# The values of chunk 0 first, from rows that are scaled but not shifted, with the shift's share added to KV as z times a row

## The chip, the cores and the metric

The kernel runs on one core of one Trainium2 chip. The metric is the device time of one launch, in microseconds (us). Every run also has a span, which is what the profiler saw and is about 1.8 us shorter, and a mean granted TensorE clock, where 1.0 is full speed. The experiments were timed in rounds beside fresh runs of the kernel before, on the chip of their batch.

A ratio is the mean time of one kernel's fast runs over the mean time of the other's fast runs of the same rounds. It is therefore not quite the ratio of the medians that are quoted.

Engines are called as the profile calls them: PE is TensorE (matmul), DVE is VectorE, ACT is ScalarE, POOL is GpSimd, SP is SyncE, which issues most of the DMA here.

## The reference, cut to what matters

```python
mod = (silu(c) @ w_mod).reshape(1, 6, 1, 1024)
sa, ca, ga, sb, cb, gb = ...                 # six rows of 1024
h = layernorm(x) * (1 + ca) + sa             # x: 2048 x 1024, "scale" ca and "shift" sa
q, k, v = h @ wqkv                           # 32 heads of 32
pq, pk = phi(q), phi(k)                      # phi(t) = where(t > 0, t + 1, exp(t)) + 1e-6
kv = einsum('bhsd,bhse->bhde', pk, v)        # per head 32 x 32, summed over all rows
z  = einsum('bhsd->bhd', pk)
o  = (pq @ kv) / (pq . z + 1e-6)
x  = x + ga * (o @ wo)
# then a second layernorm with cb, sb and a SwiGLU block of width 3584 (about 70% of PE's busy time)
```

The kernel works on four chunks of 512 rows, of four tiles of 128 rows each. A "group" is one 128 x 512 block of outputs: eight matmuls of 512 columns, one for each block of 128 inputs (`cc`). A chunk's keys are eight groups, and so are its values and its queries. I write K(2) for the keys of chunk 2, and so on.

## The kernel before: what the change and the argument touch

The loads are queued in the order in which the opening needs them. Keys come first, so the opening needs both scale and shift, of six of the eight blocks of columns, before any main matmul.

```python
    for k in range(DC // MP):                      # w_mod: scale (q=1) and shift (q=0), 768 of 1024 columns
        load_a(k, 1, nc.scalar if k == 0 else nc.sync)
        load_a(k, 0, nc.sync)
    # ... then wk, the fourth x tile, the other columns of w_mod, wv, x of chunk 1, wq
```

A tile's statistics run on DVE, its power of −1/2 and the small product `nmr` on POOL, the normalisation on ACT. The vector, scalar and POOL instructions of the opening are held in the order in which they are written:

```python
    def rstd_of(mv, n):
        # ... veps on DVE
        nc.gpsimd.tensor_tensor(out=rstd[:, 0:n], in0=veps[:, 0:n], in1=neg_half[:]..., op=ALU.pow)

    def normalise_act(dst, src, mv, rstd):
        # nmr = -mean * rstd on POOL, then
        nc.scalar.activation(out=dst, in_=src, func=ACT.Identity, bias=nmr[:], scale=rstd[:, 0:1])

    with in_order(nc.vector, nc.scalar, nc.gpsimd):
        # ...
        st0 = ln1_stats(0, 0)
        nc.vector.tensor_copy(out=sc32[:], in_=...)
        xns = [ln1_norm(*st0)] + [ln1_norm(*ln1_stats(0, t)) for t in range(1, 3)]
        # ... row products of scale and shift, transposes of three tiles, modulation of six blocks
        k_mms(0, gs, accs, 0, 5)                   # 30 main matmuls
        xn3 = ln1_norm(*ln1_stats(0, 3), dve=True)
        pe_transpose_tile(hT, xn3, 3)
        # ...
        k_mms(0, gs, accs, 5, A)
        mod_cols_b()                               # the other two blocks, 32 matmuls of one column
        # ... the rest of K(0)
```

The rest of the attention is a loop over chunks:

```python
    for sc in range(NSC):
        if sc > 0:
            k_phase(sc, 0, 2)
            kv_phase(sc - 1)                       # kvp: 128 small matmuls
            k_phase(sc, 2, 4)
            # ...
        v_phase(sc)
        if sc + 1 < NSC:
            with tc.issue_after(last_on[nc.vector.engine] if sc == 0 else last_phi[-5].ins):
                ln1(sc + 1)                        # next chunk; its tiles are transposed by DMA into hT
        # ...
    K_STEPS = [(), (2, 3), (0, 2), (0, 2, 4, 6)]   # behind which K groups a piece of the later modulation
    V_STEPS = [0, 4, 4, 6]                         # rows is summed on DVE, and how many during V
```

## Time and profile before

| | before |
|---|---|
| time, median of 3 (range) | 833.67 us (832.79 to 833.79) |
| span, granted clock | 831.0 us, 1.00 |
| last load that the first main matmul waits for | lands at 14.23 us |
| first main matmul (K of chunk 0) | 15.59 us |
| Q(0), V(1), V(2) start | 44.49, 73.38, 102.55 us |

From the page of the kernel before, first the busy time of each engine, then the chain of work that ended last by engine:

```profile
PE 819.9 (99%) x4502; PEld 378.9 (46%) x4581; DVE 344.5 (41%) x659; ACT 168.5 (20%) x253; POOL 64.3 (8%) x166
...
PE 97%; DMA 2%; issue 1%; DVE 0%; ACTq 0%; SPq 0%
```

PE is the limit everywhere except at the very start. So a change to the opening gains what it takes from the first 15.6 us, and any matmul added later costs its own length.

The chain of waits of the kernel before, in its first 19 us (start, length, what), shows what the opening waits for:

```profile
7.83 6.40 DMA wme<-in_w_mod_dram
14.23 0.04 issue
14.28 0.51 PE mod_ps L98 x8
14.79 4.21 PE acc L98 x19
```

It is a load of w_mod. After the last row products come four matmuls of zeros (1.04 us from 14.72) that keep PE busy while DVE modulates, and from 15.59 us the main matmuls follow one another. Here are the stages in PE's timeline of the kernel before (start, length, engine, line, operation, out<-in, size, count, and in brackets idle time before it):

```profile
15.59 6.64 PE L98 MATMUL acc<-wk,hT 128*128 128x512 bf16 x29
22.07 0.61 PE L101 MATMUL tp<-ident,xn 128*128 128x128 bf16 x8
...
44.49 13.98 PE L98 MATMUL acc<-hT,wq 128*128 128x512 bf16 x62
...
73.38 13.98 PE L98 MATMUL acc<-wv,hT 128*128 128x512 bf16 x62
87.19 3.75 PE L98 MATMUL acc<-wk,hT 128*128 128x512 bf16 x16
...
102.55 13.98 PE L98 MATMUL acc<-wv,hT 128*128 128x512 bf16 x62
```

None of these lines has idle time in brackets. The 30 matmuls from 15.59 us (one record is missing) hide the statistics and the normalisation of tile 3, whose transposes start at 22.07 us.

### The profile page before, as it was taken

Reading aid. Unit: us, or ns where it says so; the run is one execution under the profiler, and the core shown is the slowest. Engines: PE = TensorE matmul, PEld = TensorE weight load, DVE = VectorE, ACT = ScalarE, POOL = GpSimd, SP = SyncE. Lnnn points to the kernel's source line nnn. Section 1 sums busy time; section 2 is a strip of 40 time slices with the busy share of each in tenths; the row PEclk is TensorE's granted clock in tenths of the full one; section 3 lists DMA queues with packets and bytes.
Section 4 is the critical chain, followed back from the end, with each engine's and each line's share of the span. In section 5 each row is a group of like instructions: output and inputs, shape, how many; then the busy total and the mean of one; then the engine's idle time right before and its main releaser. Section 6 shows DMA issues by size and latency. Waiting matters only on the chain.

```text
span 831.0 us, 11112 instructions
## 1 busy us (share of the span) xinstructions
PE 819.9 (99%) x4502; PEld 378.9 (46%) x4581; DVE 344.5 (41%) x659; ACT 168.5 (20%) x253; POOL 64.3 (8%) x166
## 2 busy tenths in 40 slices
PE   8999999999999999999999999999999999999998
PEld 4444444444444444444444444444444444444444
DVE  5758879786354335421111354111114431111122
ACT  3455343434111111101111010111111101111000
POOL 2101020120221101100000010000001100000000
PEclk9999999999999999999999999999999999999999
DMA  9893964149986735646343183763405529710011
GB/s 324 296 203 65 194 150 102 37 101 326 375 204 219 227 121 169 160 153 211 110 146 108 54 221 92 249 195 100 153 1 174 152 68 345 231 45 0 19 58 51
DMA packets 144100, 129.07 MB, mean 155 GB/s; under 512 B 58608, under 2 KB 124656, under 8 KB 143536
## 3 DMA queue, kind: packets, MB, share of 16 engines
q1 hardware_dynamic: 139968, 114.97, 46.8%
q0 software_dynamic: 3792, 12.98, 4.9%
q8 instruction: 36, 0.59, 0.3%
q10 hardware_dynamic: 288, 0.40, 0.1%
q14 instruction: 16, 0.13, 0.0%
HBM read 101.98 MB, written 12.72 MB: 138 GB/s over the span
## 4 chain that ended last, share of the span: by engine, by line
PE 97%; DMA 2%; issue 1%; DVE 0%; ACTq 0%; SPq 0%
PE acc L98 90%; PE a_ps L98 7%; DMA wme<-in_w_mod_dram 2%; PE kvp L98 1%; PE wf L98 0%; PE den L98 0%; PE mod_ps L98 0%; ACTq L126 0%; PE tp L101 0%; SPq L135 0%; DVE e L698 0%; DVE ob L701 0%
## 5 line engine op out<-in xcount | busy, mean ns | idle before, releaser
L98 PE MATMUL acc<-h2T,wgu 128*128 128x512 bf16 x1755 | 385.6, 379 | 1.9
L98 PEld LDWEIGHTS <-wgu 128*128 128x128 bf16 x1792 | 175.3, 98 | 211.3
L677 DVE TENSOR_TENSOR gu<-acc,e 128x512 bf16<-128x512 f32 x112 | 77.4, 691 | 289.9 <-PE acc L98 278.8
L98 PE MATMUL acc<-wd,gu 128*128 128x512 bf16 (+2 forms) x908 | 195.2, 372 | 0.9
L676 ACT ACTIVATE e<-acc 128x512 f32<-128x512 f32 x112 | 66.9, 597 | 374.8 <-PE acc L98 363.4
L98 PEld LDWEIGHTS <-gu 128*128 128x128 bf16 x924 | 89.3, 98 | 104.4
L98 PEld LDWEIGHTS <-hT 128*128 128x128 bf16 x512 | 49.6, 98 | 59.8 <-DVE hT L237 0.9
L698 DVE TENSOR_TENSOR e<-acc,gb_bc 128x512 f32<-128x512 f32 (+2 forms) x33 | 22.3, 675 | 131.5 <-PE acc L98 122.5
L98 PE MATMUL a_ps<-wo,pq 128*128 128x512 bf16 x250 | 56.9, 379 | 0.3
L98 PE MATMUL acc<-wk,hT 128*128 128x512 bf16 x251 | 56.4, 379 | 0.5 <-issue 0.3
L98 PE MATMUL acc<-hT,wq 128*128 128x512 bf16 x249 | 55.8, 379 | 0.7 <-issue 0.5
L98 PE MATMUL acc<-wv,hT 128*128 128x512 bf16 x249 | 55.5, 379 | 0.4
L295 ACT ACTIVATE eb<-acc 128x512 bf16<-128x512 f32 x64 | 37.9, 596 | 75.4 <-PE acc L98 73.3
L234 ACT ACTIVATE xn<-x,nmr,rstd 128x1024 bf16<-128x1024 f32 x16 | 19.9, 1241 | 126.0 <-POOL nmr L232 126.0
L98 PEld LDWEIGHTS <-pq 128*128 128x128 bf16 x256 | 25.0, 98 | 30.2
L645 POOL DMA_DIRECT2D x_scratch<-x x16 | 9.8, 615 | 373.8 <-DVE x L638 373.6
L98 PEld LDWEIGHTS <-wq 128*128 128x128 bf16 x256 | 24.6, 98 | 29.8 <-issue 0.9
L296 DVE TENSOR_SCALAR eb<-eb 128x512 bf16<-128x512 bf16 x64 | 18.3, 290 | 31.2 <-ACT eb L295 31.0
L218 POOL TENSOR_TENSOR rstd<-veps,neg_half 128x1 f32<-128x1 f32 x32 | 17.8, 557 | 102.3 <-DVE veps L216 92.3
L638 DVE TENSOR_TENSOR x<-a_ps,x_sb 128x512 f32<-128x512 f32 x32 | 22.1, 690 | 8.6 <-PE a_ps L98 7.9
L701 DVE TENSOR_TENSOR ob<-e,x1r 128x512 bf16<-128x512 f32 (+2 forms) x33 | 22.3, 675 | 1.0
L639 DVE BATCH_NORM_STATS2 stats<-x 128x6 f32<-128x512 f32 x32 | 22.1, 693 | 1.0
(92 smaller groups left out, 295.9 us busy)
## 6 DMA issues: line engine op xcount, KB each, us to landing
wgu<-in_B_w_gate_dram SPq DMA_DIRECT2D x28, 1024.0 KB, 7.5
wgu<-in_B_w_up_dram SPq DMA_DIRECT2D x28, 1024.0 KB, 8.1
x_sb<-in_A_x_dram SPq DMA_DIRECT2D x32, 256.0 KB, 5.5
x_scratch<-x POOLq DMA_DIRECT2D x16, 512.0 KB, 3.4
x1r<-x_scratch SPq DMA_DIRECT2D x31, 256.0 KB, 2.7
wd<-in_B_w_down_dram SPq DMA_DIRECT2D x7, 1024.0 KB, 6.3
rbc<-rden_scratch POOLq DMA_DIRECT2D x16, 256.0 KB, 5.5
out_dram<-ob SPq DMA_DIRECT2D x31, 128.0 KB, 1.7
```

The source lines that it names most:

```text
L98: return tc.keep_in_program_order(nc.tensor.matmul(out, lhsT=lhsT, rhs=rhs, start=start, stop=stop))
L218: nc.gpsimd.tensor_tensor(out=rstd[:, 0:n], in0=veps[:, 0:n], in1=neg_half[:].to_broadcast([P, n]), op=ALU.pow)
L234: nc.scalar.activation(out=dst, in_=src, func=ACT.Identity, bias=nmr[:], scale=rstd[:, 0:1])
L295: nc.scalar.activation(out=e[:], in_=acc, func=ACT.Exp)
L296: nc.vector.tensor_scalar(out=e[:], in0=e[:], scalar1=1.0, scalar2=PHI_EPS, op0=ALU.min, op1=ALU.add)
L638: nc.vector.tensor_tensor(out=x1[:, ns], in0=a_ps[:], in1=x_t[:, ns], op=ALU.add)
L639: nc.vector.bn_stats(out=stats[:, nb, :], in_=x1[:, ns])
L645: nc.gpsimd.dma_start(out=x1_dram[st * P:(st + 1) * P, :], in_=x1[:])
L676: nc.scalar.activation(out=sg[:], in_=ps[0][:], func=ACT.Silu)
L677: gm = nc.vector.tensor_tensor(out=guT[sc][f // GPT][:, f % GPT, :], in0=ps[1][:], in1=sg[:], op=ALU.mult)
L698: nc.vector.tensor_tensor(out=yt, in0=y_ps, in1=gb_bc[:, ns], op=ALU.mult)
L701: nc.vector.tensor_tensor(out=ob, in0=yt, in1=x1r, op=ALU.add)
```

## The change

The values of chunk 0 come first. For them the rows are only scaled, `hs = xn * (1 + ca)`, so the opening needs half of w_mod's two blocks before its first main matmul. What is missing in V is the same row `vb = sa @ wv` on every line. In `kv = pk^T V` it adds up to `z0` times `vb`, where `z0` is the sum of `pk` over chunk 0. That is added to KV near 150 us. Keys and queries of chunk 0 use fully modulated rows as before.

The diff, cut to its core:

```diff
+    for j in range(DC):
+        load_block(wca, wm_v, j, D, nc.scalar if j == 0 else nc.sync)      # scale, 2.1 MB
+    for cc in range(DC):
+        load_block(wv, wqkv_v, cc, 2 * D)                                  # x tiles 2 and 3 in between
+    # ... shift (wsa), two x tiles of chunk 1, wk by blocks, the other two x tiles, wq
@@
-        st0 = ln1_stats(0, 0)
+        st0, st1 = ln1_stats(0, 0), ln1_stats(0, 1)
         nc.vector.tensor_copy(out=sc32[:], in_=...)
-        xns = [ln1_norm(*st0)] + [ln1_norm(*ln1_stats(0, t)) for t in range(1, 3)]
+        xn0, xn1 = ln1_norm(*st0), ln1_norm(*st1, dve=True)
@@
+        # ... row products of the scale, transposes of tiles 0 and 1
+        scale_to(hs, hT, 0, 0, H)                     # H: two tiles now, three before
+        # ... blocks 1 to 3
+        xn2 = ln1_norm(*ln1_stats(0, 2))
+        # ... blocks 4 to 7
+        gs = k_groups[0:4]
+        v_mms(hs, gs, accs, 0, 6)                     # 24 main matmuls
+        pe_transpose_tile(hT, xn2, 2)
+        for cc in range(DC):
+            scale_to(hs, hT, cc, H, H + P)
+        xn3 = ln1_norm(*ln1_stats(0, 3))
+        v_mms(hs, gs, accs, 6, DC)                    # 8 of them
+        v_mms(hs, gs2[0:1], accs2[0:1])               # 8 more
+        v_evac(0, gs, accs)
+        pe_transpose_tile(hT, xn3, 3)
+        for cc in range(DC):
+            scale_to(hs, hT, cc, H + P, SCW)
+        v_mms(hs, gs2[1:2], accs2[1:2])
+        mod_rows(0, 0, DC)                            # row products of the shift
+        # ... two more groups of V, then modulate_all(hT, ca1T, saT)
@@
-        v_phase(sc)
+        if sc == 0:
+            k_phase(0, 0, 8)
+        else:
+            v_phase(sc)
@@
     kv_phase(NSC - 1)
-    nc.vector.tensor_copy(out=KVB, in_=kv_acc[:, :, 0:DH])
+    vb = acc_b("vb", (HG, DH))
+    for cc in range(DC):
+        row_matvec(vb[:]..., sc32[:, cc, :], wv[cc // 4][:, cc % 4, :], cc == 0, cc == DC - 1)
+    # ... zb = vb * z0
+    nc.vector.tensor_tensor(out=KVB, in0=kv_acc[:, :, 0:DH], in1=zb, op=ALU.add)
```

(The folds of wo that follow are moved by one group of queries.)

More of the change, by code (lines that the diff above doesn't have):

```diff
@@ L122, in load_x @@
         x_tiles[st] = x_sb
-    for st in range(STC - 1):
+    for st in range(2):
         load_x(st, nc.sync)
     nc.scalar.dma_start(out=c_sb[:], in_=c_v)
-    wk = [big("wk", [4, D]), big("wk", [4, D])]
-    A, MP = 6, 2
-    AW, BW = A * P, (DC - A) * P
-    wma = [big("wme", [MP, 2, AW]) for _ in range(DC // MP)]
-    wmb = big("wme", [DC, 2, BW])
-    def load_a(k, q, eng):
-        eng.dma_start(out=wma[k][:, :, q, :], in_=wm_v[:, k * MP:(k + 1) * MP, q * D:q * D + AW])
-    def load_b(q, lo, hi):
-        nc.sync.dma_start(out=wmb[:, lo:hi, q, :], in_=wm_v[:, lo:hi, q * D + AW:(q + 1) * D])
@@ L140, in load_k @@
-    def load_k(cc):
-        nc.sync.dma_start(out=wk[cc // 4][:, cc % 4, :], in_=wqkv_v[:, cc, D:2 * D])
-    for k in range(DC // MP):
-        load_a(k, 1, nc.scalar if k == 0 else nc.sync)
-        load_a(k, 0, nc.sync)
-    load_k(0)
-    load_k(1)
-    load_x(STC - 1, nc.sync)
-    for cc in range(2, A):
-        load_k(cc)
-    for q in (1, 0):
-        load_b(q, 0, DC // 2)
-        load_b(q, DC // 2, DC)
-    for cc in range(A, DC):
-        load_k(cc)
-    def load_w(view, lo, name):
-        ts = []
-        for h in range(2):
-            t = big(name, [4, D])
-            nc.sync.dma_start(out=t[:], in_=view[:, 4 * h:4 * h + 4, lo:lo + D])
-            ts.append(t)
-        return ts
@@ L165, with load_block @@
-    wv = load_w(wqkv_v, 2 * D, "wv")
-    for st in range(STC, 2 * STC):
-        load_x(st, nc.sync)
-    wq = load_w(wqkv_v, 0, "wq")
+    wv = [big("wv", [4, D]) for _ in range(2)]
+    wca = [big("wme", [4, D]) for _ in range(2)]
+    wsa = [big("wme", [4, D]) for _ in range(2)]
+    wk = [big("wk", [4, D]) for _ in range(2)]
+    def load_block(tiles, view, cc, lo, eng=nc.sync):
+        eng.dma_start(out=tiles[cc // 4][:, cc % 4, :], in_=view[:, cc, lo:lo + D])
+    for j in range(DC):
+        load_block(wca, wm_v, j, D, nc.scalar if j == 0 else nc.sync)
@@ new lines @@
+    for cc in range(DC):
+        load_block(wv, wqkv_v, cc, 2 * D)
+        if cc in (0, 2):
+            load_x(2 + cc // 2, nc.sync)
+    for j in range(DC):
+        load_block(wsa, wm_v, j, 0)
+    for st in range(STC, STC + 2):
+        load_x(st, nc.sync)
+    for cc in range(DC):
+        load_block(wk, wqkv_v, cc, D)
+    for st in range(STC + 2, 2 * STC):
+        load_x(st, nc.sync)
+    wq = [big("wq", [4, D]) for _ in range(2)]
+    for h in range(2):
+        nc.sync.dma_start(out=wq[h][:], in_=wqkv_v[:, 4 * h:4 * h + 4, 0:D])
@@ L174 @@
     base_t = ep.tile([P, NB], BF16, name="eb")
-    base = base_t[:, 0:A * 64].rearrange("p (i q r) -> p i q r", q=2, r=32)
-    nc.gpsimd.memset(base[:, :, 0, :], 0.0)
-    nc.gpsimd.memset(base[:, :, 1, :], 1.0)
+    MW = DC * DH
+    nc.gpsimd.memset(base_t[:, 0:MW], 1.0)
     scT = const.tile([P, DC], BF16, name="scT")
@@ L185 @@
     scr_t = ep.tile([P, NB], F32, name="e")
-    scr = scr_t[:, 0:A * 64].rearrange("p (i q r) -> p i q r", q=2, r=32)
-    sa0T, ca0T = scr[:, :, 0, 0], scr[:, :, 1, 0]
+    scr = scr_t[:].rearrange("p (q i r) -> p q i r", q=2, r=DH)
+    ca0T = scr[:, 1, :, 0]
     sbT = const.tile([P, DC], F32, name="sbT")
@@ L195 @@
     gb_bc = const.tile([P, D], BF16, name="gb_bc")
-    kvs = k8.tile([P, HG * (2 * DH + 1)], F32, name="kvs", tag="k8")
+    kvs = k8.tile([P, HG * (2 * DH + 2)], F32, name="kvs", tag="k8")
     kv_acc = kvs[:, 0:HG * (DH + 1)].rearrange("p (g e) -> p g e", e=DH + 1)
-    kvb = kvs[:, HG * (DH + 1):].bitcast(BF16)
+    z0 = kvs[:, HG * (2 * DH + 1):].unsqueeze(2)
+    kvb = kvs[:, HG * (DH + 1):HG * (2 * DH + 1)].bitcast(BF16)
     KVB = kvb[:, 0:HG * DH].rearrange("p (g e) -> p g e", e=DH)
@@ L268, in ln1, with by_group, row_matvec, mod_rows @@
             ln1_norm(*ln1_stats(sc, t))
-    def mod_rows_a(k):
-        for j in range(k * MP, (k + 1) * MP):
-            rows = wma[k][:, j % MP, :, :].rearrange("p q (i r) -> p i q r", r=P)
-            for g in range(4):
-                mm(mod_ps[32 * g:32 * g + 32, 0:A * 64], lhsT=sc32[:, j, :], rhs=rows[:, :, :, 32 * g:32 * g + 32],
-                   start=False, stop=(j == DC - 1))
-    def mod_turn(lo, hi):
-        nc.vector.transpose(out=scr_t[:, lo * 64:hi * 64], in_=mod_ps[:, lo * 64:hi * 64])
-    def mod_cols_b():
-        cb = mod_ps[:, NB - 2 * (DC - A):NB]
-        mm(cb, lhsT=ident[:], rhs=base_t[:, 32 - (DC - A):32 + (DC - A)], start=True, stop=False)
-        for q in (1, 0):
-            for j in range(DC):
-                for i in range(DC - A):
-                    col = q * (DC - A) + i
-                    mm(cb[:, col:col + 1], lhsT=wmb[:, j, q, i * P:(i + 1) * P], rhs=scT[:, j:j + 1],
-                       start=False, stop=(q == 0 and j == DC - 1 and i == DC - A - 1))
-        nc.vector.tensor_copy(out=sca[:, :, A:DC], in_=cb.rearrange("p (q i) -> p q i", q=2))
+    def by_group(rows, g):
+        return rows.rearrange("p (i r) -> p i r", r=P)[:, :, g * DH:(g + 1) * DH]
+    def row_matvec(out, lhsT, rows, start, stop):
+        for g in range(4):
+            mm(out[g * DH:(g + 1) * DH, :], lhsT=lhsT, rhs=by_group(rows, g), start=start, stop=stop)
+    def mod_rows(q, lo, hi):
+        for j in range(lo, hi):
+            row_matvec(mod_ps[:, q * MW:(q + 1) * MW], sc32[:, j, :], (wsa, wca)[q][j // 4][:, j % 4, :],
+                       q == 0 and j == 0, j == DC - 1)
+    def mod_turn(lo, hi):
+        nc.vector.transpose(out=scr_t[:, lo * DH:hi * DH], in_=mod_ps[:, lo * DH:hi * DH])
+    def scale_to(hs, hT, cc, lo, hi):
+        nc.vector.tensor_scalar(out=hs[:, cc, lo:hi], in0=hT[:, cc, lo:hi], scalar1=ca0T[:, cc:cc + 1], scalar2=None,
+                                op0=ALU.mult)
     last_phi = [None]
@@ L321, in k_phase, with v_mms, v_evac @@
             mod_step(int(k_groups.index(g) in K_STEPS[sc]))
+    def v_mms(hT, gs, accs, cc_lo=0, cc_hi=DC):
+        for cc in range(cc_lo, cc_hi):
+            for (t, nb), acc in zip(gs, accs):
+                mm(acc[:], lhsT=hT[:, cc, t * P:(t + 1) * P], rhs=wv[cc // 4][:, cc % 4, nb * NB:(nb + 1) * NB],
+                   start=(cc == 0), stop=(cc == DC - 1))
+    def v_evac(sc, gs, accs):
+        for (t, nb), acc in zip(gs, accs):
+            nc.scalar.copy(out=vs[sc][:, t * D + nb * NB:t * D + (nb + 1) * NB], in_=acc[:])
     def v_phase(sc):
@@ L326, in v_phase @@
         nc.gpsimd.memset(v[:, VT:], 1.0)
-        for t in range(STC):
-            for nb in range(NNB):
-                acc = acc_a()
-                for cc in range(DC):
-                    mm(acc[:], lhsT=hTs[sc][:, cc, t * P:(t + 1) * P],
-                                     rhs=wv[cc // 4][:, cc % 4, nb * NB:(nb + 1) * NB],
-                                     start=(cc == 0), stop=(cc == DC - 1))
-                nc.scalar.copy(out=v[:, t * D + nb * NB:t * D + (nb + 1) * NB], in_=acc[:])
+        for g in k_groups:
+            acc = acc_a()
+            v_mms(hTs[sc], [g], [acc])
+            v_evac(sc, [g], [acc])
     def q_phase(sc, lo=0, hi=DC, steps=0):
@@ L360, in kv_phase @@
             nc.vector.tensor_copy(out=kv_acc, in_=kvv)
+            nc.vector.tensor_copy(out=z0, in_=kv_acc[:, :, DH:DH + 1])
         else:
@@ L478, in keep_warm_f32 @@
             mm(acc[:, 0:zeros.shape[1]], lhsT=zeros[:, 0:P], rhs=zeros, start=True, stop=True)
-    gs = k_groups[0:6]
-    accs = [acc_a() if i < 4 else acc_b("acc") for i in range(6)]
-    spare = accs[5]
+    accs = [acc_a() for _ in range(4)]
+    spare = accs[3]
     keep_warm_f32(spare, 3)
@@ L485 @@
     hT = hTs[0] = big("hT", [DC, SCW])
-    pks[0] = big("pk", [STC, D])
-    H = 3 * P
+    hs = big("hs", [DC, SCW])
+    vs[0] = big("v", [VT + DH])
+    nc.gpsimd.memset(vs[0][:, VT:], 1.0)
+    H = 2 * P
     with in_order(nc.vector, nc.scalar, nc.gpsimd):
         mod_ps = acc_b("mod_ps")
-        mm(mod_ps[:, A * 64:A * 64 + DC], lhsT=c_sb[:], rhs=ident[0:DC, 0:DC], start=True, stop=True)
+        mm(mod_ps[:, 0:DC], lhsT=c_sb[:], rhs=ident[0:DC, 0:DC], start=True, stop=True)
         for g in range(4):
-            mm(mod_ps[32 * g:32 * g + 32, 0:A * 64], lhsT=ident[:, 0:32], rhs=base_t[:, 0:A * 64],
-               start=True, stop=False)
-        nc.scalar.activation(out=scT[:], in_=mod_ps[:, A * 64:A * 64 + DC], func=ACT.Silu)
-        st0 = ln1_stats(0, 0)
-        nc.vector.tensor_copy(out=sc32[:], in_=scT[:].unsqueeze(2).to_broadcast([P, DC, 32]))
-        xns = [ln1_norm(*st0)] + [ln1_norm(*ln1_stats(0, t)) for t in range(1, 3)]
-        keep_warm_f32(spare, 3)
-        mod_rows_a(0)
-        pe_transpose_tile(hT, xns[0], 0)
+            mm(mod_ps[g * DH:(g + 1) * DH, MW:2 * MW], lhsT=ident[:, 0:DH], rhs=base_t[:, 0:MW], start=True, stop=False)
+        nc.scalar.activation(out=scT[:], in_=mod_ps[:, 0:DC], func=ACT.Silu)
+        st0, st1 = ln1_stats(0, 0), ln1_stats(0, 1)
+        nc.vector.tensor_copy(out=sc32[:], in_=scT[:].unsqueeze(2).to_broadcast([P, DC, DH]))
+        xn0, xn1 = ln1_norm(*st0), ln1_norm(*st1, dve=True)
+        keep_warm_f32(spare, 1)
         for h in range(2):
@@ L505 @@
             nc.scalar.copy(out=sc_row[:, h * NB:(h + 1) * NB], in_=accs[h][:])
-        mod_rows_a(1)
-        pe_transpose_tile(hT, xns[1], 1)
-        keep_warm(spare, 2)
-        pe_transpose_tile(hT, xns[2], 2)
-        mod_rows_a(2)
-        keep_warm(spare, 5)
-        mod_rows_a(3)
-        keep_warm(spare, 4)
-        mod_turn(0, 1)
-        modulate(hT, 0, ca0T, sa0T, 0, P)
-        modulate(hT, 0, ca0T, sa0T, P, H)
-        mod_turn(1, A)
-        for cc in range(1, A):
-            modulate(hT, cc, ca0T, sa0T, 0, H)
@@ L520 @@
-        nc.vector.tensor_copy(out=sca[:, :, 0:A], in_=scr[:, :, :, 0].rearrange("p i q -> p q i"))
-        k_mms(0, gs, accs, 0, 5)
-        xn3 = ln1_norm(*ln1_stats(0, 3), dve=True)
-        pe_transpose_tile(hT, xn3, 3)
-        for cc in range(A):
-            modulate(hT, cc, ca1T, saT, H, SCW)
-        k_mms(0, gs, accs, 5, A)
-        mod_cols_b()
-        gs7, accs7 = k_groups[6:7], [acc_b("acc")]
-        k_mms(0, gs7, accs7, 0, A)
-        for cc in range(A, DC):
-            modulate(hT, cc, ca1T, saT)
@@ L532 @@
-        k_mms(0, gs + gs7, accs + accs7, A, DC)
-        gs8, accs8 = k_groups[7:8], [acc_b("acc")]
-        k_mms(0, gs8, accs8)
-        k_evac(0, gs, accs)
-        k_evac(0, gs7, accs7)
-        k_evac(0, gs8, accs8)
+        keep_warm(spare, 3)
+        mod_rows(1, 0, 3)
+        pe_transpose_tile(hT, xn0, 0)
+        keep_warm(spare, 3)
+        mod_rows(1, 3, 5)
+        pe_transpose_tile(hT, xn1, 1)
+        keep_warm(spare, 3)
+        mod_rows(1, 5, DC)
+        keep_warm(spare, 3)
+        mod_turn(DC, DC + 1)
@@ new lines @@
+        scale_to(hs, hT, 0, 0, H)
+        mod_turn(DC + 1, 2 * DC)
+        for cc in range(1, 4):
+            scale_to(hs, hT, cc, 0, H)
+        xn2 = ln1_norm(*ln1_stats(0, 2))
+        for cc in range(4, DC):
+            scale_to(hs, hT, cc, 0, H)
+        gs = k_groups[0:4]
[5 more added lines that the diff above has]
+        v_mms(hs, gs, accs, 6, DC)
@@ new lines @@
+        gs2, accs2 = k_groups[4:6], [acc_b("acc") for _ in range(2)]
+        v_mms(hs, gs2[0:1], accs2[0:1])
+        v_evac(0, gs, accs)
+        pe_transpose_tile(hT, xn3, 3)
+        for cc in range(DC):
+            scale_to(hs, hT, cc, H + P, SCW)
+        v_mms(hs, gs2[1:2], accs2[1:2])
+        mod_rows(0, 0, DC)
+        mod_turn(0, DC)
+        nc.vector.tensor_copy(out=sca[:], in_=scr[:, :, :, 0])
+        v_evac(0, gs2, accs2)
+        for g in k_groups[6:8]:
+            acc = acc_a()
+            v_mms(hs, [g], [acc])
+            v_evac(0, [g], [acc])
@@ L538 @@
+        modulate_all(hT, ca1T, saT)
+        nc.vector.tensor_copy(out=sc32[:], in_=saT.unsqueeze(2).to_broadcast([P, DC, DH]))
     with tc.issue_after(last_on[nc.gpsimd.engine]):
@@ L587 @@
     kv_phase(NSC - 1)
-    nc.vector.tensor_copy(out=KVB, in_=kv_acc[:, :, 0:DH])
+    vb = acc_b("vb", (HG, DH))
+    for cc in range(DC):
+        row_matvec(vb[:].rearrange("p g e -> p (g e)"), sc32[:, cc, :], wv[cc // 4][:, cc % 4, :], cc == 0, cc == DC - 1)
     nc.vector.tensor_tensor(out=Zden[:], in0=kv_acc[:, :, DH:DH + 1].to_broadcast([P, HG, DH]),
                             in1=zmask[:], op=ALU.mult)
+    zb_t = ep.tile([P, NB], F32, name="e")
+    zb = zb_t[:, 0:HG * DH].rearrange("p (g e) -> p g e", e=DH)
+    nc.vector.tensor_tensor(out=zb, in0=vb[:], in1=z0.to_broadcast([P, HG, DH]), op=ALU.mult)
+    nc.vector.tensor_tensor(out=KVB, in0=kv_acc[:, :, 0:DH], in1=zb, op=ALU.add)
     def fold_wo(h, nb):
@@ L600, in fold_wo @@
             (nc.scalar.copy if g % 2 == 0 else nc.vector.tensor_copy)(out=wo[h][:, g, ns], in_=ps[g][:])
-    q_phase(1, 2, 4)
+    q_phase(1, 2, 5)
     tpk = acc_b("tp", (2, P), BF16)
@@ L606 @@
     nc.vector.tensor_copy(out=KVT, in_=tpk[:])
-    q_phase(1, 4, 5)
+    q_phase(1, 5, 6)
     den_sum(0, acc_a())
@@ L610 @@
     den_spread(0)
-    q_phase(1, 5, 7)
+    q_phase(1, 6, 8)
     fold_wo(0, 1)
-    q_phase(1, 7, 8)
-    q_phase(2, 0, 1)
+    q_phase(2, 0, 2)
     fold_wo(1, 0)
-    q_phase(2, 1, 3)
+    q_phase(2, 2, 4)
     fold_wo(1, 1)
@@ L705, in down @@
                         side.pop(0)()
-    q_phase(2, 3, 4)
+    q_phase(2, 4, 5)
     with tc.issue_after(last_phi[0].ins):
@@ L710 @@
     with tc.issue_after(applied.ins):
-        q_phase(2, 4, 6)
+        q_phase(2, 5, 7)
     for st in range(STC):
         wo_tile(st)
-    q_phase(2, 6, 8)
+    q_phase(2, 7, 8)
     nc.vector.tensor_scalar_add(out=cb1T[:], in0=cbT[:], scalar1=1.0)
```

## The prediction

> **What bounds it now.** The chain of waits is TensorE for 97% of an 831.0 us span; DMA is 2%. From 15.6 us on, the timeline shows the main matmuls back to back (0.216 us per 512 columns). So only the opening can give time, and work added to PE later costs its own length.
>
> **The opening before.** The last of the modulation loads (3.9 MB of x and w_mod are needed) lands at 14.23 us by the chain; the first K matmul starts at 15.59. DMA is saturated until 36 us (the windows: 284 to 362 GB/s up to 8 us, then mostly 390 to 400). [...]I use 395. K and V of chunk 0 end at 44.66 us.
>
> **What the change removes.** The first matmul now needs two x tiles and 2.1 MB of scales: 2.62 MB. The windows' running total reaches that at 9.6 us; loads before land about 1.3 us behind the total, so the last scale block lands near 10.7 and the first V matmul starts near 11.9. Gain 3.7 us. wv arrives about as fast as four groups use it (0.86 us a block).
>
> **What it adds on PE.** The transposes of tile 2 now stand between main matmuls (+0.5 us). The shift's row products (32 matmuls of 256 columns, estimate 1.0 us from 0.51 us for two blocks of 384) replace the column products (0.94 us by the timeline): about 0. The same product again for vb, late: +1.0 us.
>
> **A new wait.** Call t the end of tile 2's transposes on PE, near 17.9 us. Vector work is held in order: copy 0.69, eight scalings of 128 columns at 0.24, then the statistics of tile 3 (1.65), pow and nmr (0.9 with gaps), the normalisation on ACT (1.24): tile 3's rows are ready at t + 6.6. PE has only 16 matmuls (3.45 us) before it wants to transpose them. It should stand idle about 3.1 us, from about 21.3 to 24.5. (Before, 30 matmuls hid it.) Then: transposes 0.6, one group 1.7, shift rows 1.0, two groups 3.5, so K starts near 31.3 us. By then wk has landed (estimate 29.4) and cc 0 is modulated; K takes 13.85, so V and K end near 45.2, 0.5 us later than before. ln1 of chunk 1 now shares DVE with the evacuation of K, hidden by four accumulators.
>
> **Sum.** -3.7 + 0.5 + 0 + 3.1 + 1.0 = about +1, a little more with small waits on wv[...]: time 835.2 us; range 832.6 to 837.4. Chances: faster by over 2% 0.01, within 2% 0.98, slower by over 2% 0.01.
>
> **What would show it.** First main matmul at 11.3 to 12.5 us. A wait of PE for xn from ACT of 2.5 to 3.5 us near 21 to 24. No wait for wk. End of chunk 0's K between 44.5 and 46. vb: 32 matmuls in 0.9 to 1.2 us near 150, no idle around KVB. From there the two traces the same, shifted.
>
> **What would make it wrong.** The granted clock may drop: [...]no part of this trace shows it (granted clock 1.00). [...]If the vector work of tile 3 runs sooner than I read, the stall shrinks, the loads of wk bind instead, and the kernel gains up to 1 to 2 us. If wv or wk come later than the running total suggests, PE waits there, but partly instead of the stall.

## More of the kernel before

POOL's timeline of the kernel before shows how the first tile's small work goes:

```profile
5.12 0.57 POOL L218 TENSOR_TENSOR rstd<-veps,neg_half 128x1 f32<-128x1 f32 x1 [3.19 <-DVE veps L216]
5.79 0.37 POOL L232 TENSOR_SCALAR nmr<-mv,rstd 128x1 f32<-128x1 f32 x1
```

The power and the product of tile 0 follow directly on one another.

## The result, and the profile after

The changed kernel gives the right result. Its median is 837.09 us (836.16 to 838.22, 4 runs), against 833.5 us of the kernel before (832.79 to 833.79, 4 runs). The ratio is 1.0045, with a 95% interval of 1.0028 to 1.0062. The interval lies clear of 1: the kernel became about 3.7 us slower. The prediction was 835.2 us, with a range to 837.4.

The profiled run of the changed kernel is one of 838.22 us, with a span of 836.4 us and a mean clock of 0.998. From its page, the two lines that answer to those above:

```profile
PE 826.5 (99%) x4609; PEld 378.8 (45%) x4609; DVE 348.7 (42%) x679; ACT 168.2 (20%) x253; POOL 64.0 (8%) x165
...
PE 95%; DVE 2%; DMA 1%; ACT 1%; issue 1%; POOL 0%; ACTq 0%; DVEq 0%; POOLq 0%
```

The chain now has DVE and ACT in it. PE's timeline of the changed kernel says where:

```profile
12.97 5.35 PE L98 MATMUL acc<-wv,hs 128*128 128x512 bf16 x24
...
24.88 0.62 PE L101 MATMUL tp<-ident,xn 128*128 128x128 bf16 x8 [2.66 <-ACT xn L218]
25.34 3.52 PE L98 MATMUL acc<-wv,hs 128*128 128x512 bf16 x8
...
47.06 13.98 PE L98 MATMUL acc<-hT,wq 128*128 128x512 bf16 x64
...
90.19 4.37 PE L98 MATMUL acc<-wk,hT 128*128 128x512 bf16 x16 [0.27 <-DVE hT L221]
...
98.98 8.36 PE L98 MATMUL acc<-wk,hT 128*128 128x512 bf16 x38 [1.01 <-issue]
...
154.46 1.07 PE L98 MATMUL vb<-wv,sc 128*32 128x256 bf16 x32
```

Four things are to be seen. The main matmuls start 2.6 us earlier (12.97 against 15.59). PE then stands 2.66 us for tile 3. The eight matmuls after that wait take 3.52 us, though eight of them take 1.89 us elsewhere. And in K(2) there is new lost time: the first 16 matmuls take 4.37 us and wait 0.27 us for hT, and a later gap of 1.01 us is put down to nothing ("issue").

The chain of waits of the changed kernel shows the stall for tile 3 as it was predicted, one vector instruction behind the other:

```profile
18.81 0.70 DVE hT L228
...
19.54 1.39 DVE hs L270 x8
20.93 1.20 DVE stats L208 x2
...
23.59 1.25 ACT xn L218
```

The slow matmuls after the stall are a matter of clock. These are the windows of the changed kernel in steps of 2 us (stretch, length, busy time and count of PE, PEld, DVE, ACT, POOL, then the granted clock, the DMA share and GB/s):

```profile
22.00:24.00 2.00, 0.23 (x2) 0.00 (x0) 0.49 (x3) 0.41 (x1) 1.26 (x7) 1.00 1.05 386
24.00:26.00 2.00, 1.12 (x10) 0.71 (x11) 0.46 (x1) 2.00 (x4) 1.24 (x32) 0.86 1.06 388
26.00:28.00 2.00, 2.00 (x6) 0.76 (x5) 1.63 (x9) 1.25 (x3) 0.00 (x0) 0.50 1.05 386
28.00:30.00 2.00, 2.00 (x36) 0.86 (x34) 0.09 (x1) 0.59 (x1) 0.00 (x0) 0.79 1.05 388
```

PE is idle through nearly all of the first stretch, and soon after it the granted clock is 0.50 for 3.41 us (25.44 to 28.85). Two of the four runs have a mean clock of 0.998, the others 0.999 and 1.0, so this happens in some runs and not in others.

At the start POOL's timeline of the changed kernel differs from that of before:

```profile
5.33 0.57 POOL L202 TENSOR_TENSOR rstd<-veps,neg_half 128x1 f32<-128x1 f32 x1 [3.56 <-DVE veps L200]
6.95 0.56 POOL L202 TENSOR_TENSOR rstd<-veps,neg_half 128x1 f32<-128x1 f32 x1 [1.05 <-DVE veps L200]
7.49 0.26 POOL L216 TENSOR_SCALAR nmr<-mv,rstd 128x1 f32<-128x1 f32 x1
```

The product `nmr` of tile 0 now stands behind the power of tile 1, since both tiles' statistics are written ahead of both normalisations. It comes at 7.49 us, where it was at 5.79 us before. The normalisation of tile 0 starts at 7.79 us and its transposes at 9.09 us. PE waits 1.45 us for them, while the loads are not what it waits for.

### The profile page after: what moved, and what is told of

Same layout as the page of the kernel before. It is cut to its first block, busy times and chain, and to the rows that moved or that the text cites. A ratio compares the mean times of both kernels' runs of the same rounds, so it can differ in the third digit from the quotient of the medians.

```text
span 836.4 us, 11281 instructions
## 1 busy us (share of the span) xinstructions
PE 826.5 (99%) x4609; PEld 378.8 (45%) x4609; DVE 348.7 (42%) x679; ACT 168.2 (20%) x253; POOL 64.0 (8%) x165
## 4 chain that ended last, share of the span: by engine, by line
PE 95%; DVE 2%; DMA 1%; ACT 1%; issue 1%; POOL 0%; ACTq 0%; DVEq 0%; POOLq 0%
PE acc L98 87%; PE a_ps L98 7%; DVE stats L208 1%; PE kvp L98 1%; DMA hT<-xn 1%; ACT xn L218 0%; POOL rstd L202 0%; DMA x_sb<-in_A_x_dram 0%; PE tp L101 0%; DVE wmt L400 0%; DVE pk L280 0%; PE mod_ps L98 0%; PE wf L98 0%; PE den L98 0%; DVE hs L270 0%
## 5 line engine op out<-in xcount | busy, mean ns | idle before, releaser
L702 DVE TENSOR_TENSOR e<-acc,gb_bc 128x512 f32<-128x512 f32 (+2 forms) x33 | 22.3, 675 | 131.7 <-PE acc L98 128.8
L98 PEld LDWEIGHTS <-hT 128*128 128x128 bf16 x448 | 43.4, 98 | 54.8 <-DVE hT L221 2.4
L98 PE MATMUL acc<-wv,hT 128*128 128x512 bf16 x192 | 41.9, 379 | 0.0
L218 ACT ACTIVATE xn<-x_sb,nmr,rstd 128x1024 bf16<-128x1024 bf16 x15 | 18.4, 1238 | 21.5 <-POOL nmr L216 21.5
L705 DVE TENSOR_TENSOR ob<-e,x1r 128x512 bf16<-128x512 f32 (+2 forms) x33 | 22.3, 675 | 1.0
```

Of the source, the lines that this page charges most:

```text
L98: return tc.keep_in_program_order(nc.tensor.matmul(out, lhsT=lhsT, rhs=rhs, start=start, stop=stop))
L702: nc.vector.tensor_tensor(out=yt, in0=y_ps, in1=gb_bc[:, ns], op=ALU.mult)
L705: nc.vector.tensor_tensor(out=ob, in0=yt, in1=x1r, op=ALU.add)
```

## The experiments

**Theory.** (1) The stall for tile 3 is the vector queue's order and not a load. (2) The start is held up by POOL's order. (3) The slow matmuls come from a drop of the granted clock after a long gap of PE. (4) The loss in K(2) hangs on when the transposed rows of chunk 2 are ready. **Rivals.** The stall and the start are bound by loads (wv and wk, or the scale). The slow matmuls come from mixing tile shapes or operands. The loss in K(2) belongs to the change itself, by the vb product or the new order of V and K.

The first four kernels ran on one chip, beside nine runs of the kernel before with a median of 833.68 us.

### The changed kernel again (ctl_after)

No edit.

> The changed kernel again, on the chip of the other three runs. Theory: about 3.6 us slower than the kernel before (ratio near 1.0045); tile 3's transposes wait about 2.7 us for the normalisation on ACT, and [...]the granted clock halves for about 3.4 us afterwards, which should be the reason why single runs spread over 2 us. Rival (the extra products on PE are the loss, the wait is hidden by later slack): nothing to tell here. The 1.0 us gap on PE at 98 us and the late hT of chunk 2 either recur (then they belong to the change) or not (then they are chance).

Measured: 836.66 us (835.89 to 837.89, 5 runs), ratio 1.0040 (1.0027 to 1.0052). Three runs have a clock of 1.0 and two of 0.998. The profiled run is one without a drop, span 834.6 us. Its PE timeline:

```profile
13.07 5.35 PE L98 MATMUL acc<-wv,hs 128*128 128x512 bf16 x24
...
24.98 0.62 PE L101 MATMUL tp<-ident,xn 128*128 128x128 bf16 x8 [2.65 <-ACT xn L218]
25.43 1.89 PE L98 MATMUL acc<-wv,hs 128*128 128x512 bf16 x8
...
45.52 13.98 PE L98 MATMUL acc<-hT,wq 128*128 128x512 bf16 x63
...
88.70 4.38 PE L98 MATMUL acc<-wk,hT 128*128 128x512 bf16 x16 [0.32 <-DVE hT L221]
...
97.19 8.36 PE L98 MATMUL acc<-wk,hT 128*128 128x512 bf16 x38 [0.69 <-issue]
105.38 13.98 PE L98 MATMUL acc<-wv,hT 128*128 128x512 bf16 x62
```

What follows: the same wait of 2.65 us is there without the slow matmuls (1.89 us), so the drop is not a certain consequence of the wait. (The gaps with a drop and those without are set side by side under e11.) Over this batch and the first one, the four runs at 0.998 have a mean of 837.73 us and the five at 0.999 or 1.0 have 836.34 us, so a drop costs about 1.4 us. The loss in K(2) is there again, without a drop. This run without a drop is the one to set against the kernel before, stage by stage (V(1) from its timeline at 74.41 us, the first queries after KV at 153.89, the first matmul of the SwiGLU block at 208.02):

| first matmul of | before | changed, no drop | behind by | since the line above |
|---|---|---|---|---|
| main matmuls | 15.59 | 13.07 | −2.5 | −2.5 |
| Q(0) | 44.49 | 45.52 | +1.0 | +3.5 |
| V(1) | 73.38 | 74.41 | +1.0 | 0 |
| V(2) | 102.55 | 105.38 | +2.8 | +1.8 |
| queries after KV | 150.18 | 153.89 | +3.7 | +0.9 |
| SwiGLU | 204.32 | 208.02 | +3.7 | 0 |

Tenths in the first line are not firm: the same opening starts its main matmuls at 12.84 to 13.29 us in the eight traces that have it, and that of the kernel before at 15.59 and, in e9 below, 15.17.

### Statistics of tile 3 earlier (e1_stats3_early)

```diff
+        xn3 = ln1_norm(*ln1_stats(0, 3))
         gs = k_groups[0:4]
         v_mms(hs, gs, accs, 0, 6)
         pe_transpose_tile(hT, xn2, 2)
         for cc in range(DC):
             scale_to(hs, hT, cc, H, H + P)
-        xn3 = ln1_norm(*ln1_stats(0, 3))
```

> Statistics and normalisation of tile 3 moved ahead of tile 2's scalings in the held order; nothing else. Theory (the wait is a matter of order): tile 3's rows are ready near 20.5 us, PE has no wait for xn at 22, no drop of the granted clock, K of chunk 0 starts near 29 instead of 33.2, and the time falls by 3 to 4.4 us against the changed kernel, to about the kernel before (832.5 to 834). Rival (the loads bind there: wsa or wk come too late): PE waits about as long for wme at 24.5 or wk at 29 as it waited for xn, and the time falls by under 1.5 us.

Measured: 836.12 us (835.14 to 838.08), ratio 1.0034 (1.0021 to 1.0046). The stall is gone and K(0) starts at 28.80 us, where the clean run of the changed kernel has 31.71. PE waits for no load in between, so the stall was the order and not wv. But the time hardly moved. The gain is given back in K(0), as DVE's timeline of this kernel shows, followed by PE's:

```profile
36.62 0.69 DVE L208 BATCH_NORM_STATS2 stats<-x_sb 128x6 f32<-128x512 bf16 x1 [3.77 <-DMA x_sb<-in_A_x_dram]
37.23 0.48 DVE L278 TENSOR_SCALAR eb<-eb 128x512 bf16<-128x512 bf16 x2
```

```profile
38.36 1.44 PE L98 MATMUL acc<-wk,hT 128*128 128x512 bf16 x3 [2.49 <-DVE pk L280]
```

The statistics of chunk 1 stand in the vector queue ahead of the evacuation of K(0), and one of them waits 3.77 us for an x tile. That tile was issued at 27.55 us and landed at 36.6, while 2 MB of wq were being moved too. Meanwhile the accumulators fill up and PE waits 2.49 us. In the clean run of the changed kernel that tile lands at the same time (36.55 us), but DVE comes to it later, by the stall, and waits for it only 0.79 us. So the stall at tile 3 hid this wait. The granted clock fell to 0.56 and 0.59 in the two stretches of 2 us from 38 us on, where this wait ends. My expectation in time failed; its part about the stall held.

### The first row's chain first (e2_row0_first)

```diff
-        st0, st1 = ln1_stats(0, 0), ln1_stats(0, 1)
+        xn0 = ln1_norm(*ln1_stats(0, 0))
         nc.vector.tensor_copy(out=sc32[:], in_=...)
-        xn0, xn1 = ln1_norm(*st0), ln1_norm(*st1, dve=True)
+        xn1 = ln1_norm(*ln1_stats(0, 1), dve=True)
```

> Tile 0's normalisation and the copy sc32 traced before tile 1's statistics, so that the pow of tile 1 no longer stands before the nmr of tile 0 on POOL; tile 3's order as in the changed kernel. Theory (the start is bound by the chain x0, x1, pow, nmr, xn0 and the matmuls queued behind tile 0's transposes, not by the scale loads): first V matmul at 11.2 to 11.6 instead of 12.97 us, everything after shifted, time 1.2 to 1.7 us below the changed kernel. Rival (the scale loads set the start, as the prediction had it): first V matmul no earlier than 12.5, time within 0.5 us.

Measured: 836.5 us (835.5 to 837.5), ratio 1.0036 (1.0023 to 1.0048). The first main matmul is at 12.11 us, 0.96 us earlier than in the clean run, and there is no wait for the first tile. The time is inconclusive: three of the five runs are at 0.998, against two of the control's, and a drop costs more than this edit gains. What follows is that POOL's order cost about 1 us at the start, as theory (2) says: the four traces with tile 0's chain first (this one, and e5 to e7) start at 11.70 to 12.11, the eight with the order of the changed kernel at 12.84 to 13.29. The 11.2 to 11.6 us that I expected was not reached.

### Matmuls of zeros in the stall (e3_warm_in_wait)

```diff
         v_evac(0, gs, accs)
+        keep_warm(accs2[1], 12)
         pe_transpose_tile(hT, xn3, 3)
```

> Twelve idle-filling matmuls on a free accumulator (2.6 us) before tile 3's transposes: the wait for tile 3 stays, but PE is busy in it. Theory (the wait is paid twice, once as idle and once as a halved clock after it): granted clock 1.00 throughout, the eight matmuls after the transposes take 1.73 us instead of 3.35, K of chunk 0 ends about 1.7 us earlier in the profile; mean time 0.5 to 1.7 us below the changed kernel and with less spread. Rival (the clock view is an artefact and costs nothing): no change of the time, within 0.3 us, or slower by what the fillers overrun.

Measured: 838.22 us (837.6 to 839.6), ratio 1.0063 (1.0049 to 1.0077). In the profiled run the clock stays at 1.00 there, the next eight matmuls take 1.89 us and Q(0) starts at 45.43 us, all as expected. But it is slower than the changed kernel, so my expectation in time failed. V(2) starts at 106.58 us, 1.2 us later than in the clean run: the gap at KV(1) is now 1.64 us (0.69 there), and K(2) starts after a wait of 0.63 us (0.32 there). Two of the five runs still have a clock of 0.998, and I have no profile of those. So the filler did what it was to do where it stands, and something else grew.

The next three kernels ran on another chip, beside nine runs of the kernel before with a median of 833.6 us.

### The next chunk's statistics held back too (e4_ln1_held)

e1 and:

```diff
-            with tc.issue_after(last_on[nc.vector.engine] if sc == 0 else last_phi[-5].ins):
+            with tc.issue_after(last_phi[-5].ins):
                 ln1(sc + 1)
```

> The early statistics of tile 3 as in e1, and the statistics of chunk 1 held until the first evacuations of K of chunk 0 have been traced (as the later chunks have it). Theory (e1 removed the wait for tile 3, but gave the gain back because the vector queue then stood 3.8 us for the x tile that lands at 36.6 behind 2 MB of wq, so that K's accumulators were not emptied): no wait of PE for the evacuation near 36, the first Q matmul at 42.9 to 43.3 us instead of 45.5 (clean) or 46.9 (e1), time 2 to 3 us below the changed kernel's clean runs, near 833.5 to 834.5; runs with a granted clock of 0.998 gone or rare, since no wait over 2 us is left. Rival (the loads bind whatever the order): PE waits elsewhere near 30 to 40 us and the time stays above 835.5.

Measured: 832.82 us (832.64 to 834.05), ratio 0.9998 (0.9986 to 1.0011). All five runs have a clock of at least 0.999. PE's timeline:

```profile
28.81 13.98 PE L98 MATMUL acc<-wk,hT 128*128 128x512 bf16 x63
42.62 13.98 PE L98 MATMUL acc<-hT,wq 128*128 128x512 bf16 x63
```

K(0) now runs without a wait, and Q(0) starts 2.9 us earlier than in the clean changed run. Against the control's ratio this is 0.0042, or about 3.5 us. That includes the drops in two of the control's five runs (1.4 us each, 0.6 us in the mean). This settles theory (1): the stall for tile 3 is worth its whole length once the x tile is no longer ahead of the evacuation. It also settles what e1 lost. The changed kernel is then as fast as the one before, and not faster, although Q(0) starts 1.9 us earlier than it (42.62 against 44.49). By V(2) that is lost (103.02 against 102.55): in K(2) PE waits 0.52 us for its rows, its first 16 matmuls take 4.38 us, and a gap of 1.02 us follows. The five runs lie at 832.6 to 832.8 and 834.0 to 834.1 us, and the profile is of one of the slower two.

### The start too (e5_start_too)

e4 and e2 together.

> e4 with tile 0's normalisation and sc32 ahead of tile 1's statistics (the edit of e2). Theory (with the wait gone, the next bound is the loads of wk, whose last block lands near 30.3 us): V starts 0.9 us earlier (12.1), but K, group by group, needs all of wk in its first group, so PE waits near 29 and most of the 0.9 us is lost: first Q matmul 0 to 0.5 us before that of e4, time within 0.6 us of e4. Rival (the start passes through in full): first Q matmul 0.9 us earlier, time 0.9 us lower.

Measured: 833.2 us (833.06 to 833.53), ratio 0.9997 (0.9984 to 1.0011). The first main matmul is at 11.70 us, but Q(0) starts at 42.45, only 0.17 us earlier than in e4. The 24 first matmuls take 5.80 us instead of 5.35, for which the profile names no cause (in e6 and e7, with the same opening, they take 5.37 and 5.35), and K(0) waits for its weights, as PE's timeline has it:

```profile
30.15 12.46 PE L98 MATMUL acc<-wk,hT 128*128 128x512 bf16 x56 [0.29 <-DMA wk<-in_A_wqkv_dram]
```

So the rival is right here and only here: with both orders mended, the loads of wk bind, and the earlier start brings next to nothing by itself. That wv binds too is not shown.

### The vb product early (e6_vb_early)

e5, with the product done between V(0) and K(0), where PE waits for wk, and its result kept in SBUF:

```diff
+        nc.vector.tensor_copy(out=sc32[:], in_=saT...)       # behind the shift's columns
         v_evac(0, gs2, accs2)
         # ... the last two groups of V
+        vb = acc_b("vb", (HG, DH))
+        for cc in range(DC):
+            row_matvec(vb[:]..., sc32[:, cc, :], wv[cc // 4][:, cc % 4, :], cc == 0, cc == DC - 1)
         modulate_all(hT, ca1T, saT)
+        nc.vector.tensor_copy(out=vbs, in_=vb[:])
```

> e5 with the product of the shift with wv done between V and K of chunk 0 instead of at 153 us, its result kept in the tile of kv. Theory (the product costs PE 0.9 us where it stands now and nothing in the wait for wk): first Q matmul as in e5 or up to 0.5 us later, nothing at 153, time 0.5 to 0.9 us below e5, at or just under the kernel before (832.5 to 833.5). Rival (wk does not bind, as the rival of e5 has it): the product moves and costs the same, time equal to e5 within 0.3 us.

Measured: 833.25 us (832.82 to 833.51), ratio 0.9998 (0.9985 to 1.0010). The product is free there: Q(0) starts at 42.46 us with it, where e5 has 42.45 without (by chance the first 24 matmuls took 5.37 us here and 5.80 there, which gives the product part of its room). It is no longer in the chain at 150 us, so I expected 0.5 to 0.9 us. Nothing came of it, and PE's timeline shows where it went:

```profile
86.69 4.38 PE L98 MATMUL acc<-wk,hT 128*128 128x512 bf16 x16 [1.24 <-DVE hT L222]
...
116.44 4.37 PE L98 MATMUL acc<-wk,hT 128*128 128x512 bf16 x16
...
132.26 13.98 PE L98 MATMUL acc<-wv,hT 128*128 128x512 bf16 x62
```

PE waits 1.24 us for the rows of chunk 2, where e5 waits 0.44, but the gap after KV(1) (0.70 us in e5) is not there, and V(2) starts at 102.52 us as it does in e5 (102.51). The loss comes in K(3): DVE waits 2.10 us for the transposes of chunk 3 and modulates its rows from 115.88 us (113.78 in e5), the first 16 matmuls take 4.37 us instead of 3.62, and V(3) starts at 132.26 us, where e5 has 131.40. So what is saved at 150 us has been lost before it to the rows of the next chunk, at K(3) and not only at the K(2) of theory (4). The expectation in time failed.

The next three ran on a third chip, beside nine runs of the kernel before with a median of 833.08 us.

### Two pieces of vector work later (e7_all_steps_late)

e6 and:

```diff
-    K_STEPS = [(), (2, 3), (0, 2), (0, 2, 4, 6)]
-    V_STEPS = [0, 4, 4, 6]
+    K_STEPS = [(), (), (0, 2), (0, 2, 4, 6)]
+    V_STEPS = [0, 6, 4, 6]
```

Two of the six pieces of 1.2 to 1.3 us that DVE sums for the later modulation move from K(1) to V(1), behind the statistics of chunk 2.

> e6 with the two ga sums that stood between K's evacuations of chunk 1 done after that chunk's statistics instead (four become six). Theory (what is left against the kernel before is lost at K of chunk 2, whose rows arrive from the DMA transpose 1.2 us after PE wants them, and the transposes wait for a vector queue that these sums hold up by 2.4 us): no wait of PE for hT at 86, the first group of K of chunk 2 takes 3.6 us for 16 matmuls and not 4.4, V of chunk 2 starts at 100.6 to 101 us instead of 102.5, time 831 to 832, below the kernel before by 0.2 to 0.3 per cent. Rival (the transposes are late for a reason in the DMA queues, not for their start): wait unchanged, time within 0.4 us of e6.

Measured: 831.34 us (830.99 to 831.51), ratio 0.9977 (0.9964 to 0.9989). This version beats both kernels, by little. The waits of PE in the first 240 us are one line, the wait for zeros at the very start:

```profile
PE acc L98 <- DVE sel L459: 1.2, 1, 1.2
```

Its PE timeline at K(2) and V(2):

```profile
85.55 3.88 PE L98 MATMUL acc<-wk,hT 128*128 128x512 bf16 x16
...
100.89 13.98 PE L98 MATMUL acc<-wv,hT 128*128 128x512 bf16 x64
```

V(2) is 1.6 us earlier than in e6 and V(3) 2.1 us (130.14 against 132.26), and that is the gain in time (0.9998 less 0.9977, times 833.5 us: 1.75 us; the spans of the profiled runs differ by 2.1). The last normalisation of chunk 2 ends at 78.55 us, 6.8 us after V(1) started (71.73). In e6 it ended 8.1 us after it (79.56 and 71.47). So the rows are normalised, and then transposed, sooner. The order of V and K and the vb product are as in the changed kernel or e6, and the loss in K(2) is gone; so it doesn't follow from them alone, and that rival falls.

### The same edit on the changed kernel, and on the kernel before (e8_after_steps_late, e9_before_steps_late)

> The changed kernel with this edit alone. Theory: K of chunk 2 no longer waits for its rows (0.3 to 0.4 us of wait and 0.76 us of pacing gone), time 0.8 to 1.8 us below the changed kernel's 836.7; the wait for tile 3 and the halved clock after it in some runs stay. Rival: no change.

Measured: 836.98 us (835.46 to 837.09), ratio 1.0045 (1.0032 to 1.0059). Four of the five runs are at 0.997 or 0.998, so the time is inconclusive. The profiled run, at 0.999, has a span of 833.7 us against 834.6 of the clean control. Its first 16 matmuls of K(2) take 3.88 us without a wait, and V(2) starts at 104.43 us against 105.38. The gap of PE after KV(1) stays (0.73 us). Counted from V(1) (74.27 against 74.41), the edit takes away 0.8 us, the part that hangs on hT.

> The kernel before with this edit alone, as a control: there the first group of K of chunk 2 loses only 0.13 us to its rows (3.75 us for 16 matmuls), so the edit is worth at most 0.2 us: time 833.2 to 833.8. If it gains 1 us or more, the late rows are not a loss of the changed kernel but of both.

Measured: 833.63 us (833.56 to 833.97), ratio 1.0005 (0.9993 to 1.0018). The kernel before gains nothing from it: there hT was in time already (the first 16 matmuls took 3.75 us, now 3.88). A gap of 1.04 us after KV(1) appears instead, which the profiled run of the kernel before does not have. So that gap is not a property of the change.

The last two ran on that chip, too, beside eleven runs of the kernel before with a median of 833.47 us.

### Does the drop follow a gap, whatever its place? (e10_zeros_again, e11_data_in_wait)

e10 is e3 again. e11 has real data in the same twelve matmuls:

```diff
         v_evac(0, gs, accs)
+        for _ in range(12):
+            mm(accs2[1][:], lhsT=hs[:, 0, 0:P], rhs=wv[0][:, 0, 0:NB], start=True, stop=True)
         pe_transpose_tile(hT, xn3, 3)
```

> The kernel of e3 again, to see where its runs with a granted clock of 0.998 (two of five) lose it. Theory A (the wait causes the drop and fillers cure it): then a drop in this kernel lies elsewhere, after another gap of PE. Theory B [...]: a drop, where the profile falls on one, lies at 25 to 29 us as in the changed kernel.

Measured: 837.34 us (836.58 to 837.9), ratio 1.0045 (1.0032 to 1.0058), all five runs at a clock of 1.0. The gap is there again (1.66 us).

> The changed kernel with twelve fillers in the wait for tile 3 that multiply real data (hs by wv, result overwritten later) instead of zeros. Theory A: as e3, still some runs at 0.998. Theory B: no run at 0.998, all five near the clean level of e3 (837.6) or of the changed kernel (836.3). If drops stay here too, the wait for tile 3 is not their only cause, and that stays open.

Measured: 837.69 us (836.83 to 840.45, 6 runs), ratio 1.0055 (1.0042 to 1.0068). The clocks are 0.998, 1.0, 1.0, 1.0, 0.999 and 1.0. The profiled run is the one of 840.45 us. Its clock is 1.00 where the stall of tile 3 was, and the drop is elsewhere. PE's timeline of e11, then its windows (columns as above):

```profile
93.65 1.20 PE L98 MATMUL kvp<-v,pk 128*32 128x64 bf16 x126
97.24 0.21 PE L98 MATMUL kvp<-v,pk 128*32 128x64 bf16 x2 [2.39 <-issue]
97.38 12.22 PE L98 MATMUL acc<-wk,hT 128*128 128x512 bf16 x48
```

```profile
96.00:98.00 2.00, 0.76 (x5) 0.40 (x5) 0.43 (x1) 0.00 (x0) 0.00 (x0) 1.00 0.90 236
98.00:100.00 2.00, 2.00 (x7) 0.78 (x6) 0.00 (x0) 0.00 (x0) 0.00 (x0) 0.61 0.15 53
100.00:102.00 2.00, 2.00 (x6) 0.69 (x5) 1.33 (x3) 0.60 (x1) 0.00 (x0) 0.54 0.00 0
```

A gap of 2.39 us at another place, with other work around it, is followed by the same drop: 48 matmuls take 12.22 us instead of 10.53. So theory (3) stands and its rival falls. In the profiled runs, gaps of 2.66 (changed), 2.65 (e2), 2.49 (e1) and 2.39 us (e11) were followed by a drop; gaps of 2.65 (control) and 2.66 us (e8) were not, nor was any of 1.66 us or less. In e4 to e7, whose largest gap is 1.24 us, all 20 runs have a clock of at least 0.999.

The length of a gap does not decide alone, then, and what else decides was not shown. The drops themselves are alike. In the trace of the changed kernel the granted clock is 0.50 from 25.44 to 28.85 us, 3.41 us long, which takes away 1.71 us of full clock. The stretches of 2 us that a drop touches lose 1.70 us together in each of the other three as well: e1 has 0.56 and 0.59 in them, e2 0.97, 0.50 and 0.68, and e11 0.61 and 0.54. That is as much as 3.4 us at 0.50.

### The gap after KV(1)

The gap that the profile calls "issue" sits at a fixed place of PE's instructions. In the changed kernel, the control, e1, e2, e4, e5 and e8 it comes ten matmuls after the last of KV(1). In e3, e10 and e11, which have twelve matmuls more before it (24 instructions, with their weight loads), it comes two matmuls before the end of KV(1), twelve matmuls or 24 instructions earlier. In e9, whose stages before it have other counts, it comes six matmuls after. In the trace of the changed kernel 734 weight loads and 733 matmuls come before the gap. Its length is anything from 0.50 (e2) to 2.39 us (e11). The profile names nothing that PE waits for there.

Packets of the queue that the page calls "instruction" pass near it. In the changed kernel the fifth packet of that queue passes from 96.43 to 97.54 us, and PE goes on at 98.98, 1.44 us after its end. In windows of 0.5 us such a packet begins between 94.5 and 95.0 us in the control and between 93.5 and 94.0 in e3, and PE goes on at 97.19 and 96.07, that is 2.1 to 2.7 us after its beginning, where the changed kernel has 2.55. In the kernel before, where 734 weight loads come before 93.49 us, the fifth packet ends at 91.95 us, 1.54 us earlier, and the profile shows no wait there. So gap and packet lie close together in these traces. No run moved the packet by itself: that PE waits for it is my guess and not shown, and why some runs have the gap and others not is open.

## Why the prediction was right or wrong

The total was inside the range, 1.9 us above the forecast (837.1 against 835.2) and 0.3 us below the upper end. That is partly luck: the steps alone were off by 2.8 us (0.9 against 3.7, summed below), of which the 0.6 us that the forecast put on top for small waits took up a part. The steps, against the clean run of the changed kernel:

- **"Gain 3.7 us", first V matmul near 11.9: mis-sized.** It was 2.5 us (13.07), or 2.6 in the first profile. I took the loads as the limit and did not follow POOL's queue, where `nmr` of tile 0 comes behind the power of tile 1. That is where it was lost: with tile 0's chain written first the start came to 12.11 (e2) and 11.70 to 11.93 (e5 to e7, whose other edits lie later). No wait for a scale load shows in any of them, so the loads were in time for a start at 11.9; whether they were the next limit there is not shown.
- **Transposes of tile 2, +0.5: right.** 18.26 to 18.71 us on PE in the control is 0.45.
- **Shift rows for column products, about 0: right.** 0.99 us (27.25 to 28.24) replace 0.83 (23.81 to 24.64).
- **PE idle about 3.1 us for tile 3, from 21.3 to 24.5: right.** It was 2.65, from 22.3 to 25.0, and in the chain that I had read it from. e1 and e4 show that it was the vector order.
- **No wait for wk: right.** With the stall gone there is none either (e4); with the start mended too, wk binds (e5).
- **End of chunk 0's K at 44.5 to 46: right** in the clean run (45.52); in a run with a drop it was 47.06.
- **vb, +1.0: right.** The step in the table of stages is 0.9. It is avoidable (e6).
- **"From there the two traces the same, shifted": wrong.** K(2) lost another 1.8 us. About 1.1 of it is the rows of chunk 2: they are modulated from 88.23 us, 13.8 us after V(1) starts, where the kernel before has 12.7 (86.10 and 73.38). The normalisations end 8.08 us after the start of V(1) in both. So it is the transposes by DMA that come later: the last one is issued 9.36 us after V(1) starts instead of 8.94 (83.77 and 82.32 us), and from its issue to the modulation it is 4.46 us instead of 3.78. The 16 matmuls then go at the pace of the modulation (eight pieces in 2.67 us, paired with matmuls: 4.38 us instead of 3.75). The rest, 0.7 us in the clean run, is the gap after KV(1), which is not a property of the change (e9). I had taken the stages after the opening to have slack against a shift, and at this one there was hardly any.
- **The clock: named as a risk, and it came in about half of the runs.** The forecast did not count one in. By the runs a drop cost about 1.4 us, and in the profiled runs drops followed gaps of 2.39 to 2.66 us, shorter than the 3.1 us of idle time that the forecast had.
- **"If the vector work of tile 3 runs sooner, the kernel gains up to 1 to 2 us": half right.** Moved sooner by hand, it gained 0.5 us alone (e1) and 3.5 us with the next chunk's statistics held back (e4).

Predicted, the sum was −3.7 + 0.5 + 0 + 3.1 + 1.0 = 0.9 us. The clean run has −2.5 for the start, +3.5 up to Q(0) (2.65 for the stall, 0.45 for tile 2, 0.16 for the rows, the rest at the joints), +1.8 in K(2) and +0.9 for vb: 3.7 us, and its span is 3.6 us longer.

What stays open: why the transposes of chunk 2 are issued and land later against PE in the changed kernel; what PE waits for in the gap after KV(1), and why some runs do not have it; what decides whether a drop follows a gap of about 2.65 us; and where the two runs of e3 with a clock of 0.998 had their drop.

## What to carry to other kernels

When the loads in front of the first matmul are cut, follow every engine's queue up to that matmul, the small POOL instructions too: the order in which they are written became the next limit, and a stall further on hid another wait behind it. Mend such waits together and look at the whole trace after each, since gains in this kernel were given back twice (e1, e6), some 15 and 90 us after the place of the edit. A gap of PE can cost more than its length, so keep gaps short where nothing else can be done: here gaps of 2.39, 2.49, 2.65 and 2.66 us were followed by a granted clock near 0.50 for about 3.4 us, which cost about 1.4 us of time; two of 2.65 and 2.66 us were not, nor was any of 1.66 us or less.
